# Loading two small projection matrices over other queues: E and F by SyncE and ScalarE in f32, with casts on two engines

## The chip, the cores and the metric

The kernel runs on one core of a Trainium2 chip. A core has five engines that run side by side, each with its own stream of instructions: TensorE (PE, matrix products and transposes into PSUM; PEld is its loading of weights), VectorE (DVE), ScalarE (ACT), GpSimd (POOL) and SyncE (SP). Transfers between memory and the chip are issued by GpSimd, SyncE or ScalarE and carried out by DMA engines. The metric is the device time of one launch in microseconds (us), lower is better; the time before is 431.67 us, the median of 4 runs (431.21 to 432.22).

## The reference

The kernel computes a Linformer attention and feeds its result to an MLP-Mixer block. Sizes: batch 8, 8 heads, sequence 1024, head size 64, projected length 64; the mixer has a token width of 256 and a channel width of 1536.

```python
k_proj = np.einsum('ks,bhsd->bhkd', E, k)        # E: 64 x 1024
v_proj = np.einsum('ks,bhsd->bhkd', F, v)        # F: 64 x 1024
scores = scale * np.matmul(q, k_proj.transpose(0, 1, 3, 2))
attn = softmax(scores)
x = np.matmul(attn, v_proj)                      # heads side by side: (8, 1024, 512)
h = np.maximum(x.T @ w_tok1, 0.0) @ w_tok2       # over the sequence
u = x + h.T
out = u + np.maximum(u @ w_ch1, 0.0) @ w_ch2     # over the channels
```

All inputs and the output are f32. E and F are the same for all batches and heads, so nothing of the attention can begin before both have been loaded and transposed.

## The kernel before, in words

The kernel holds everything in bf16 on chip; GpSimd's transfers change f32 to bf16 on the way. The order of the work on all engines is written out by hand in a long list of step names (ORDER); the program sorts its steps by that list and emits them, so each engine's order is fixed. Transfers are issued ahead of that list, in the order in which the code stands.

The edit is in the opening part of the kernel (lines 184 to 245). There GpSimd issues, one after another: E into partitions 0 to 63 and F into partitions 64 to 127 of one bf16 tile, EF_sb (lines 197 and 198); then, for each of the four head pairs of batch 0, k, q and v of that pair (line 165, 256 KB each as bf16); after the first of these triples it builds the identity matrix that TensorE's transposes need (two instructions from masks.py); after the last the token weights wt1 and wt2 (lines 206 and 207), and then the channel weights and the whole q, k and v of batch 1 (lines 191, 165 and 195). A GpSimd transfer takes one of eight semaphores in turn, so the ninth waits until the first has landed, and so on.

Meanwhile VectorE clears the two block-diagonal tiles kbd and vbd (lines 216 to 219). TensorE multiplies zeros eight times to stay active (busy, line 226), and then runs the first steps of the list:

- EF: eight transposes of EF_sb into PSUM (line 231), and a copy by VectorE into EFT (line 232).
- For head pair hp: KP.hp and VP.hp, the projections of k and v by EFT (lines 240 and 245); KT.hp, the transposes of the projected k (265); QT.hp, the transposes of q (395); S, the scores (449), with their exponential on ScalarE (456); O, the product with the projected v (294), with a reciprocal and a product on VectorE (300, 301). Some KP and VP steps are preceded by filler products (line 431).
- Then the token mixing (464, 477), its transposes (491), and the channel mixing of batch 0 (532).

The copies between these steps are by VectorE or ScalarE (lines 249 and 251), by a list. ScalarE loads its table of functions ahead of its first such copy. From there the batches overlap: while TensorE does the channel mixing of one batch (lines 600 and 655), attention and token mixing of the next are inserted between. Output tiles o1 and o2 have two buffers each and are stored by SyncE (lines 676 and 680).

Of the kernel before, what the change touches and what calls it, by code (L numbers as in the profile page):

```python
# [10 lines left out]
F32 = mybir.dt.float32  # L11
BF16 = mybir.dt.bfloat16
ALU = mybir.AluOpType
ACT = mybir.ActivationFunctionType
# [78 lines left out]
def kernel(  # L93
# [13 lines left out]
    nc = tc.nc  # L107
    P = 128
    B, H, S, D = q.shape
    KP = E.shape[0]  # L110
# [13 lines left out]
    work = ctx.enter_context(tc.tile_pool(name="work", bufs=1))  # L124
# [19 lines left out]
    ident = const.tile([P, P], BF16, name="ident")  # L144
# [6 lines left out]
    kbd = const.tile([P, H, P], BF16, name="kbd")  # L151
# [8 lines left out]
    def load(b, name, src, hs=slice(0, 8)):  # L160
        if hs.start == 0:
            st[name, b] = work.tile(
                [P, H, SC * D], BF16, tag=name + "_sb", name=name + "_sb", bufs=1
            )
        nc.gpsimd.dma_start(
            out=st[name, b][:, hs], in_=src[b, hs].rearrange("h (p si) d -> p h (si d)", p=P)
        )
# [16 lines left out]
    EF_sb = work.tile([P, S], BF16, tag="T1", name="EF_sb", bufs=1)  # L184
# [9 lines left out]
        cs = slice(j * CH, j * CH + CH)  # L194
        nc.gpsimd.dma_start(out=wc2[:, cs], in_=wc2_v[:, cs])

    nc.gpsimd.dma_start(out=EF_sb[0:KP], in_=E)
    nc.gpsimd.dma_start(out=EF_sb[KP:P], in_=F)
    for hp in range(HP):
        hs = slice(2 * hp, 2 * hp + 2)  # L200
        for name, src in ((("k", k), ("q", q), ("v", v))):
            load(0, name, src, hs)
        if hp == 0:
            make_identity(nc, ident)
        if hp == 3:
            nc.gpsimd.dma_start(out=wt1, in_=moe_w_tok1.rearrange("(p si) t -> p si t", p=P))
    nc.gpsimd.dma_start(out=wt2, in_=moe_w_tok2.rearrange("(tc p) s -> p tc s", p=P))
# [13 lines left out]
    def busy(psf, n):  # L221

        zero = kbd.rearrange("p h k -> p (h k)")
        w_ps = psf("w_ps")
        for _ in range(n):
            nc.tensor.matmul(w_ps, zero[:, 0:P], zero[:, 0:512], start=True, stop=True)
# [5 lines left out]
        nc.vector.tensor_copy(out=EFT.rearrange("p s k -> p (s k)"), in_=e_ps)  # L232

    busy(c_ps, 8)


    def k_mm(b, kv_ps, hs, si, f):
# [670 lines left out]
```

## Time and profile before

| | |
|---|---|
| median of 4 runs | 431.67 us |
| the profiled execution | 431.56 us |
| its span on the core | 429.8 us |
| TensorE busy | 415.7 us, 97% of the span |
| VectorE, ScalarE, GpSimd busy | 301.6, 202.4, 206.4 us |
| granted TensorE clock | 1.0 |
| E, F: issue to landing | 3.0 and 3.1 us |

The span runs from the first to the last instruction of the core; the rest of the device time lies around it. The page gives busy time by engine, a picture of the span in 40 slices, and the chain of work that ended last, which is followed back from the last instruction to whatever released each step. In rows of the timeline, the columns are the start, the length, the engine, the line of the code, the operation, the tiles written and read, the size, the count, and in brackets the idle time of the engine before it with what ended that.

### The profile page before, as it was taken

What the parts mean: (1) busy time and instruction counts of PE and PEld (TensorE: products, weight loads), DVE (VectorE), ACT (ScalarE), POOL (GpSimd) and SP (SyncE); (2) the same over time, 40 slices, a digit from 0 to 9 for tenths busy, and PEclk for the clock granted to TensorE, in tenths of its full rate; (3) what the DMA queues carried; (4) which work ended last, traced back from release to release, by engine and by line L of the source; (5) the groups of instructions that cost most, each with busy time, mean ns of one, the idle gap of its engine ahead of it and who ended that gap; (6) DMA issues with size and microseconds to landing.
All of it is one profiled execution on the core that took longest, in us unless ns stands there. A gap on an engine that the chain in (4) does not pass through costs nothing.

```text
span 429.8 us, 7700 instructions
## 1 busy us (share of the span) xinstructions
PE 415.7 (97%) x3034; PEld 271.8 (63%) x3066; DVE 301.6 (70%) x509; ACT 202.4 (47%) x360; POOL 206.4 (48%) x150
## 2 busy tenths in 40 slices
PE   7789999999999999999999999999999999999995
PEld 3577456765478644785467844786458854785585
DVE  2475468768936878867768777777779766947862
ACT  1436684157552556234753366334652356315621
POOL 8350014134652647553565645635356626654652
PEclk9999999999999999999999999999999999999999
DMA  8999999979987999943999289364914320342014
GB/s 123 207 206 206 207 191 172 218 131 219 208 118 177 163 224 179 177 91 58 249 169 206 106 146 153 69 172 103 156 37 99 98 99 2 57 142 98 2 50 146
DMA packets 89332, 60.53 MB, mean 141 GB/s; under 512 B 55760, under 2 KB 84944, under 8 KB 89296
## 3 DMA queue, kind: packets, MB, share of 16 engines
q0 software_dynamic: 29360, 29.63, 44.2%
q1 hardware_dynamic: 59936, 30.42, 30.2%
q8 instruction: 24, 0.39, 0.4%
q14 instruction: 12, 0.10, 0.1%
HBM read 59.24 MB, written 16.78 MB: 177 GB/s over the span
## 4 chain that ended last, share of the span: by engine, by line
PE 90%; DVE 4%; DMA 2%; POOL 2%; issue 1%; ACT 0%; DVEq 0%; ACTq 0%; POOLq 0%
PE be L655 19%; PE be L600 17%; PE ga L655 9%; PE ga L600 9%; PE h_ps L341 5%; PE u_ps L357 5%; PE g_ps L532 5%; PE al L655 4%; PE al L600 4%; PE ou_ps L294 4%; PE kv_ps L240 3%; DMA q_sb<-in_q_dram 2%; PE sco L281 2%; DVE S L524 1%; PE u_ps L477 1%; PE h_ps L464 1%
## 5 line engine op out<-in xcount | busy, mean ns | idle before, releaser
L564 ACT ACTIVATE K<-be 128x512 f32<-128x512 f32 x116 | 65.7, 598 | 66.1 <-PE be L655 38.6
L655 PEld LDWEIGHTS <-g 128*128 128x128 bf16 x768 | 74.5, 98 | 16.1 <-issue 1.0
L655 PEld LDWEIGHTS <-S 128*128 128x128 bf16 x576 | 55.9, 98 | 11.7 <-issue 0.4
L286 ACT ACTIVATE attnT<-sco 128x512 bf16<-128x512 f32 x56 | 33.5, 598 | 50.9 <-PE sco L281 39.3
L600 PEld LDWEIGHTS <-wc 128*128 128x128 bf16 x336 | 32.1, 98 | 36.2 <-issue 0.4
L691 POOL TENSOR_TENSOR K<-K,u_sb 128x512 f32<-128x512 f32 x16 | 19.0, 1185 | 68.7 <-ACT K L564 68.7
L655 PE MATMUL be<-wc,g 128*128 128x256 bf16 x384 | 48.5, 273 | 0.7 <-DVE g L522 0.6
L564 ACT ACTIVATE K<-ga 128x512 f32<-128x512 f32 x58 | 33.0, 601 | 33.6 <-PE ga L655 29.9
L301 DVE TENSOR_TENSOR x_sb<-ou_ps,rdn 128x512 bf16<-128x512 f32 x64 | 44.3, 692 | 2.2
L600 PE MATMUL be<-uT,wc 128*128 128x512 bf16 x168 | 44.7, 379 | 0.2
L360 DVE TENSOR_TENSOR u_sb<-u_ps,x_sb 128x512 bf16<-128x512 f32 x56 | 37.1, 685 | 9.4 <-PE u_ps L357 8.1
L600 PEld LDWEIGHTS <-uS 128*128 128x128 bf16 x252 | 24.0, 98 | 25.7
L606 DVE CUSTOM_DVE_ANT_0 g<-be,K 128x512 bf16<-128x512 f32 x42 | 27.5, 688 | 16.8 <-PE be L600 16.6
L518 POOL TENSOR_TENSOR S<-g 128x1024 bf16<-128x1024 bf16 x7 | 14.9, 2122 | 46.7 <-DVE g L606 46.7
L522 POOL TENSOR_TENSOR g<-g 128x1024 bf16<-128x1024 bf16 x13 | 28.9, 2226 | 14.6 <-DVE S L518 14.4
L639 ACT ACTIVATE g<-be 128x512 bf16<-128x512 f32 x42 | 23.8, 597 | 25.7 <-PE be L600 25.7
L606 DVE CUSTOM_DVE_ANT_0 g<-al,K 128x512 bf16<-128x512 f32 x42 | 27.7, 688 | 10.8 <-PE al L600 10.6
L701 POOL TENSOR_TENSOR K<-K,u_sb 128x512 f32<-128x512 f32 x16 | 20.3, 1270 | 30.0 <-ACT K L564 30.0
L300 DVE RECIPROCAL rdn<-ou_ps 128x8 f32<-128x8 f32 x64 | 13.1, 205 | 25.5 <-PE ou_ps L294 25.0
L357 PE MATMUL u_ps<-R_sb,wt 128*128 128x512 bf16 x104 | 29.9, 379 | 0.6 <-DVE u_sb L360 0.3
L524 POOL TENSOR_TENSOR S<-g,S 128x1024 bf16<-128x1024 bf16 x13 | 28.3, 2183 | 0.9 <-DVE S L520 0.7
L341 PE MATMUL h_ps<-x_sb,wt 128*128 128x512 bf16 x102 | 28.1, 379 | 0.3
(101 smaller groups left out, 774.5 us busy)
## 6 DMA issues: line engine op xcount, KB each, us to landing
out_dram<-o SPq DMA_DIRECT2D x30, 512.0 KB, 3.2
q_sb<-in_q_dram POOLq DMA_DIRECT2D x7, 1024.0 KB, 12.7
k_sb<-in_k_dram POOLq DMA_DIRECT2D x7, 1024.0 KB, 12.5
v_sb<-in_v_dram POOLq DMA_DIRECT2D x7, 1024.0 KB, 12.5
wc<-in_moe_w_ch_dram POOLq DMA_DIRECT2D x4, 384.0 KB, 13.7
wc<-in_moe_w_ch_dram POOLq DMA_DIRECT2D x2, 768.0 KB, 27.4
k_sb<-in_k_dram POOLq DMA_DIRECT2D x4, 256.0 KB, 7.9
q_sb<-in_q_dram POOLq DMA_DIRECT2D x4, 256.0 KB, 8.5
```

What stands on the lines that cost most here:

```text
L286: nc.scalar.activation(out=at, in_=sco, func=ACT.Exp, scale=scale)
L301: nc.vector.tensor_tensor(out=st["x", b][:, :, h * D : (h + 1) * D].rearrange("p (b k) d -> p b k d", b=2), in0=ov[:, :, :, 0:D], in1=rdn[ ...
L341: nc.tensor.matmul(st["h", b], wt1[:, s, t * P : (t + 1) * P], st["x", b][:, s, :], start=(s == 0), stop=(s == SC - 1),)
L357: nc.tensor.matmul(u_ps, wt2[:, t, s::SC], st["R", b][:, t, :], start=(t == 0), stop=(t == TC - 1))
L360: nc.vector.tensor_add(out=st["u", b][:, s, :], in0=u_ps, in1=st["x", b][:, s, :])
L522: eng.tensor_sub(out=a21, in0=a11, in1=a21)
L524: eng.tensor_sub(out=s4, in0=a12, in1=s2)
L564: nc.scalar.activation(out=t, in_=x, func=ACT.Copy)
L600: nc.tensor.matmul(acc, l[:, dc, i * P : (i + 1) * P], r[:, :, dc, :], start=start and dc == 0, stop=stop and dc == 1, skip_group_check=True,)
L606: nc.vector._custom_dve(TENSOR_ADD_SAT, out=o, in0=x, in1=y, s0=3.0e38, s1=0.0)
L639: nc.scalar.activation(out=g_part(b, i + e, 1, 1, 0)[:, 0], in_=be[e], func=ACT.Relu)
L655: nc.tensor.matmul(acc[:, e * HF : (e + 1) * HF], l[:, lc + c, l0 + (2 * j + e) * P : l0 + (2 * j + e + 1) * P], r[:, rc + c, r0 : r0 + HF ...
```

## The change: what it does

E is no longer loaded by GpSimd but by SyncE, and F by ScalarE. Both arrive as f32 in a new tile EF_in, which takes one of the two buffers of the output tile o1. VectorE then casts the rows of E into EF_sb and ScalarE the rows of F. GpSimd begins with k of head pair 0, and builds the identity matrix after the first q instead of after the first v. ScalarE gets a copy of one element ahead of its cast. In the changed program its first instructions are: the issue of F, the load of its table, which waits for nothing, the one-element copy, which waits for the clearing of kbd, and the cast of F, which waits for F.

```diff
-    nc.gpsimd.dma_start(out=EF_sb[0:KP], in_=E)
-    nc.gpsimd.dma_start(out=EF_sb[KP:P], in_=F)
+    EF_in = work.tile([P, S], F32, tag="o1", name="EF_in", bufs=2)
+    nc.sync.dma_start(out=EF_in[0:KP], in_=E)
+    nc.scalar.dma_start(out=EF_in[KP:P], in_=F)
     for hp in range(HP):
         hs = slice(2 * hp, 2 * hp + 2)
         for name, src in ((("k", k), ("q", q), ("v", v))):
             load(0, name, src, hs)
-        if hp == 0:
-            make_identity(nc, ident)
+            if (hp, name) == (0, "q"):
+                make_identity(nc, ident)
...
     busy(c_ps, 8)
+
+    first = work.tile([P, 1], BF16, tag="first", name="first", bufs=1)
+    nc.scalar.activation(out=first, in_=kbd[:, 0, 0:1], func=ACT.Copy)
+    nc.vector.tensor_copy(out=EF_sb[0:KP], in_=EF_in[0:KP])
+    nc.scalar.activation(out=EF_sb[KP:P], in_=EF_in[KP:P], func=ACT.Copy)
```

## The prediction

> **What bounds the kernel now.** The page first: the span is 429.8 us of the profiled execution's 431.56 us, so 1.76 us lie outside it, and TensorE is busy for 415.7 us, 97% of the span, at the full granted clock. The only slices of it below nine tenths are the first three and the last. The edit touches only the first few microseconds, so I asked for the chain of work that ended last over the first 60 us (start, length, piece):
>
> ```profile
> 1.25 0.69 POOL EF_sb L197
> 1.94 0.52 POOL EF_sb L198
> 2.46 0.57 POOL k_sb L165
> ...
> 7.33 0.70 POOL k_sb L165
> 8.02 9.34 DMA q_sb<-in_q_dram
> 17.36 0.05 issue
> 17.41 0.62 PE qt_ps L395 x8
> 18.03 0.16 PE kt_ps L265 x2
> ```
>
> Up to 17.4 us the end is set by loads: GpSimd issues E, F and then the k, q and v of head pairs, and the chain sits on the transfer of the third q piece (head pair 2) until it lands at 17.36. After that it is TensorE almost without a break. So a microsecond won before 17.4 is a microsecond at the end, if TensorE can use the earlier data and nothing later takes it back.
>
> The timeline of TensorE over the same stretch says what it waits for, and with how much spare time:
>
> ```profile
> 5.27 1.01 PE L231 MATMUL e_ps<-ident,EF_sb 128*128 128x128 bf16 x8 [0.22 <-POOL ident masks.py:199]
> 7.07 1.06 PE L240 MATMUL kv_ps<-k_sb,EFT 128*64 128x128 bf16 x8 [0.78 <-DVE EFT L232]
> ...
> 12.28 0.44 PE L240 MATMUL kv_ps<-k_sb,EFT 128*64 128x128 bf16 x5 [0.82 <-DMA k_sb<-in_k_dram]
> ...
> 14.89 0.63 PE L245 MATMUL kv_ps<-v_sb,EFT 128*64 128x128 bf16 x8 [0.56 <-DMA v_sb<-in_v_dram]
> ...
> 16.16 0.61 PE L240 MATMUL kv_ps<-k_sb,EFT 128*64 128x128 bf16 x8 [0.30 <-DMA k_sb<-in_k_dram]
> ```
>
> The transposes of E and F start at 5.27 (their weight load at 5.10). From there to 17.41 TensorE stands waiting for k (0.82 + 0.30), for v (0.56) and, by its weight loads' waits, for q (0.8 in three times): 2.5 us. That is the room in which it can start later, or run earlier.
>
> Last, the stages of the transfers (stretch, then busy time and count of PE, PEld, DVE, ACT, POOL, the clock, the DMA share, GB/s as written):
>
> ```profile
> 2.00:2.50 0.50, 0.50 (x3) 0.16 (x2) 0.13 (x2) 0.50 (x1) 0.50 (x2) 1.00 0.00 0
> 2.50:3.00 0.50, 0.50 (x2) 0.15 (x1) 0.00 (x0) 0.27 (x1) 0.50 (x1) 1.00 0.63 45
> 3.00:3.50 0.50, 0.50 (x2) 0.15 (x1) 0.00 (x0) 0.00 (x0) 0.50 (x2) 1.00 0.98 147
> 3.50:4.00 0.50, 0.50 (x3) 0.16 (x2) 0.00 (x0) 0.00 (x0) 0.50 (x2) 1.00 1.17 180
> 4.00:4.50 0.50, 0.50 (x3) 0.14 (x1) 0.00 (x0) 0.00 (x0) 0.50 (x1) 1.00 1.08 178
> ```
>
> Nothing moves before about 2.65, 1.4 us after GpSimd began its first issue. E and F write 256 KB as bf16: 22 + 74 + 90 KB by 4.0, the rest at 178 GB/s by about 4.4. Only then is the stream free for the first k. From 10 us on it runs at 200 to 210 GB/s without a gap, and each 256 KB piece lands about 1.26 us after the one before it. The loads are one saturated stream, so what starts it earlier should move every landing.
>
> **What the Trainium skill says.** "DMA: Bandwidth & Descriptors", section "Specifications", puts the first byte of a GpSimd transfer at about 1 us and of a SyncE or ScalarE transfer at about 0.6 us; here GpSimd's took 1.4 with the issue, and the other is not shown on loads. The same page, "Issuing engines are not separate DMA queues", says that all of them run on the same 16 DMA engines and that issuing from several saves only sequencer time. So E and F get no bandwidth of their own; the gain can only be that they run while the engines still stand idle.
>
> **The change, part by part.**
>
> 1. *Two issues leave GpSimd* (0.69 + 0.52 us in the chain). The first k is then issued at 1.25 where E was, and data of k, q, v start at about 2.65 instead of 4.4, if E and F are out of the way: at most 1.75 us earlier. Issuing doesn't bind later: one piece costs GpSimd 0.72 us, the transfer 1.26. The wait of GpSimd for an earlier transfer still reaches back eight transfers: the third v still waits for the first k, the fourth k for the first q. Every later wait of this kind keeps its partner.
>
> 2. *E on SyncE, F on ScalarE.* Neither has work: VectorE starts its first instruction at 0.92, and SyncE and ScalarE should be free at about 0.95. SyncE's issues take 0.33 us (median of the stores), so bytes should flow from 0.95 + 0.33 + 0.6 = 1.9 at the latest, 1.55 if the 0.6 runs from the issue's start. Both move 512 KB of f32, which is the amount read before as well. At the 206 GB/s of the saturated stream as written, 412 as read, that is 1.25 us of all engines. Before 2.65 they get 0.75 to 1.1 us of that; 0.15 to 0.5 us remain and delay the first k. So the stream gains 1.75 - 0.5 = 1.25 to 1.75 - 0.15 = 1.6. If the hardware queue is slower to start than I think, E, F and k are interleaved and the gain shrinks to 0. I take 1.3, the lower part, since the early stream (147 to 180) was slower than the later one.
>
> 3. *Landing, casts and the transposes.* SyncE's stores of 512 KB (SBUF to DRAM, the only plain transfers on that queue) give the nearest landing:
>
> ```profile
> DMA to landing us min/median/max: 2.3/3.1/8.0
> ```
>
> So E and F land at about 0.95 + 3.1 = 4.05, perhaps 0.6 earlier as they are half that size. ScalarE: issue to 1.3, table load 1.28 us to 2.6 (before it waited for a memset until 1.48; now it waits for nothing), the 1-element copy, then F: a 1024-wide copy took 1.02 us here, so F is ready at 4.05 + 1.05 = 5.1. "ScalarE: Activation LUTs", "What ACT_TABLE_LOAD costs", gives 0.186 + 0.833 per thousand elements, 1.04, which agrees. VectorE: its memsets end at 2.24; E's cast costs 0.69 by the 2x column of "VectorE: DVE Perf Modes", perf-mode tier table (1.23 for 2048), or 1.2 at the slope of the PSUM casts (0.42 for 256, 0.29 for 128). Ready at 4.75 to 5.3. The identity, now built after two issues, is ready at about 3.3 instead of 5.22. So the transposes start at 4.5 to 5.4, where they start at 5.27 now: no change on this path, and no gain claimed.
>
> 4. *Whether TensorE can use it.* With the transposes as now, it is ready for the second k at 11.46, when its fillers end. That k lands at about 12.2 - 1.3 = 10.9, so this step gains 0.8. The next waits (q 0.4, v 0.56, k 0.30, q 0.2) give up the rest, and at the first step of the third q the shift is the full 1.3: 16.1 in place of 17.41. With no load to wait for it could be there at 17.41 - 2.5 = 14.9, so 1.2 us of room remain.
>
> 5. *What else is added:* the slot of an output tile holds E and F in f32; the first output tile then takes the other slot, with no wait before 79 us. The first copy into the block-diagonal k (ACT, 9.78) now also waits for ScalarE's own earlier work, done by about 5.
>
> After 17.4 TensorE's recorded waits are 3.6 us in all, all on VectorE, 2.3 of them where the attention product waits for its buffer; none is on a load. The token weights land at about 25 to 26, close to their use at 26.14, but they come in the same stream and move with it. The second batch's v lands at about 50.6 against its use at about 52. I give 0.1 for such edges.
>
> Sum: span 429.8 - 1.3 + 0.1 = 428.6; with 1.76 around it 430.36. The profiled execution is 0.11 below the median shown, so against 431.67 the forecast is **430.5**, 0.28% less. About 0.2% (0.86 us) is what a measurement of this kernel can tell from no change.
>
> **The rivals.**
>
> *No gain, the engines are shared (18%).* E's and F's packets first flow at 2.6 and interleave with k: the same bytes stand ahead of the third q, landings move by 0 to 0.6. For it: the stream already uses all 16 engines. Against it: they idle until 2.65. Time 431.1 to 431.7, say 431.4.
>
> *Gained and given back (10%).* A later wait at fixed time takes it up: VectorE's chain from the attention product, at 21.2 and 24.9. Against it: VectorE itself idles ahead of those pieces until TensorE delivers (4.6 us). Time 431.5.
>
> *Slower: E and F come late (10%).* The casts put a new step after landing. The longest landing seen on that queue is 8.0 us; at 0.95 + 8.0 + 1.05 the transposes start at 10.0, 4.7 to 4.9 late, and 2.5 us of room leave a loss of about 2.3: 434.0. It decides from transposes later than 7.7; beyond 8.5 the loss is over 0.86. A milder form: "TensorE: Matmul & The Clock Gate", Part 1, has the array at half clock after an idle window of about 3.4 us; in this trace the 512-wide fillers still take 0.43 us at 8 us and about 0.25 at 10.4, so a long gap before the transposes would add slow matmuls. About 433 for the case.
>
> *As forecast (62%):* 429.8 to 430.9 for itself.
>
> **How the numbers follow.** Faster: nearly all of the forecast's case and a little of the shared one, 0.63. Within 0.2%: most of the shared and the given-back, 0.27. Slower 0.10. The range 429.7 to 431.9 holds the forecast's case, the shared and the given-back; it leaves out the late case and a twentieth at the low end.
>
> **What would show it.** E and F landing at 3.4 to 4.1; F's cast about 1.03 us; transposes at 4.5 to 5.4; the stream at full share from about 2 us; the third q landing at 16.0 to 16.2 and TensorE's chain from 16.1, with every later piece about 1.2 earlier. Wrong if data on the new queues flow only after 2.6, if the transposes start after 7.7, or if the third q moves but not the end.

## The result, and the profile after

The changed kernel takes 430.9 us (median of 37 runs, 430.18 to 432.05) against 431.64 for the kernel before (59 runs, 430.58 to 432.42). The ratio is 0.9988, interval 0.9983 to 0.9993. By the medians that is 0.74 us, by the ratio 0.5 us: a gain clear of noise, in the direction forecast, and about half of the 1.2 us forecast (0.4 to 0.6 of it). The one profiled execution flatters it: 430.27 us, with a span of 428.5, is 1.3 us below the profiled execution before. So two things have to be explained: the 1.3 us in that execution, and why the typical run keeps only about half of it.

The chain of work that ended last, of the changed kernel, over the first 40 us (start, length, piece):

```profile
0.74 4.79 DMA EF_in<-in_E_dram
5.53 0.02 issue
5.55 0.70 DVE EF_sb L239
6.25 0.14 issue
6.38 0.70 PE e_ps L232 x8
...
8.48 1.19 PE w_ps L227 x3
...
10.86 1.52 PE kv_ps L437 x4
...
16.35 0.45 PE qt_ps L401 x8
```

The loads of k, q and v have left the chain. It now runs through the landing of E, 4.8 us after its issue, then VectorE's cast, and from 6.38 on through TensorE alone. TensorE's waits say the same, ahead of the third q (17.6 us, the whole list):

```profile
PE w_ps L227 <- DVE kbd L217: 1.5, 1, 1.5
PE e_ps L232 <- DVE EF_sb L239: 1.3, 1, 1.3
PE kv_ps L246 <- DVE EFT L233: 0.8, 1, 0.8
```

No wait for a load is left, where there were 0.82, 0.56 and 0.30 before. TensorE's timeline, and below it GpSimd's issue that waits for the third q to land:

```profile
6.38 0.69 PE L232 MATMUL e_ps<-ident,EF_sb 128*128 128x128 bf16 x8 [1.33 <-DVE EF_sb L239]
7.85 0.63 PE L246 MATMUL kv_ps<-k_sb,EFT 128*64 128x128 bf16 x8 [0.78 <-DVE EFT L233]
8.42 1.26 PE L227 MATMUL w_ps<-kbd 128*128 128x512 bf16 x3
...
10.65 1.73 PE L437 MATMUL kv_ps<-EFT,ident 128*128 128x512 bf16 x4
...
16.18 0.61 PE L401 MATMUL qt_ps<-ident,q_sb 128*128 128x128 bf16 x8
```

```profile
16.27 0.74 POOL L191 DMA_DIRECT2D wc<-in_moe_w_ch_dram  x1 [0.48 <-DMA q_sb<-in_q_dram]
```

The transposes start at 6.38 in place of 5.27, the transposes of the third q at 16.18 in place of 17.41: 1.1 later, then 1.2 earlier. In the kernel before, that issue of GpSimd began at 17.64, 0.28 after the landing at 17.36; here the third q thus landed at about 16.0, and TensorE took it up 0.2 later. Four fillers that took 1.03 us before take 1.73 here. They start 0.43 apart, where in the kernel before it was 0.22: half speed. The stretches show the clock (the number after the five engines is the granted TensorE clock, then the DMA share and GB/s written):

```profile
2.00:2.50 0.50, 0.50 (x3) 0.15 (x2) 0.13 (x2) 0.50 (x1) 0.50 (x2) 1.00 1.10 115
2.50:3.00 0.50, 0.50 (x2) 0.15 (x1) 0.00 (x0) 0.32 (x2) 0.50 (x2) 1.00 0.52 197
3.00:3.50 0.50, 0.50 (x2) 0.15 (x1) 0.00 (x0) 0.00 (x0) 0.42 (x3) 1.00 1.14 328
3.50:4.00 0.50, 0.50 (x3) 0.15 (x2) 0.00 (x0) 0.00 (x0) 0.50 (x1) 1.00 0.98 229
4.00:4.50 0.50, 0.50 (x3) 0.14 (x1) 0.00 (x0) 0.03 (x1) 0.50 (x2) 1.00 0.95 199
...
9.00:10.00 1.00, 1.00 (x6) 0.30 (x5) 0.00 (x0) 0.01 (x1) 0.46 (x2) 0.50 1.21 199
10.00:11.00 1.00, 1.00 (x9) 0.81 (x8) 0.10 (x1) 0.54 (x2) 0.63 (x1) 0.50 1.25 208
11.00:12.00 1.00, 1.00 (x4) 0.30 (x2) 0.59 (x1) 0.00 (x0) 0.72 (x1) 0.50 1.23 204
12.00:13.00 1.00, 1.00 (x18) 0.69 (x16) 0.00 (x0) 0.01 (x1) 0.57 (x1) 0.97 1.25 206
```

Two readings. From 2.0 to 4.5 about 534 KB are written, and E and F are 524 KB of f32: so they fill the engines until about 4.5, and the first k flows no earlier than before. The packets of each queue in the trace say it directly: F's run from 2.1 to 3.6, E's from 3.3 to 4.7, and the first of k moves at 4.39, where it was 4.36 in the kernel before. And the clock falls to a half from 8.7 to 12.1. It is recorded only from its first change on; the eight zero products from 1.46 ran at half speed too (0.43 us apart), though the column says 1.00 there.

The runs of the changed kernel fall in groups by their mean recorded clock: 21 of 38 with 0.995 or 0.996 take 430.18 to 430.93, 14 with 1.0 take 431.19 to 432.05, and 3 with 0.992 take 431.7 to 431.9. (One execution more has its clock on record than the 37 of the median.) A mean of 0.996 over 428.5 us is one stretch of 3.4 us at half clock, as in the profile above. A mean of 1.0 isn't a run without half clock: it only says that the clock never fell back. The half clock of the start is not counted, however long it lasts.

### The profile page after: what moved, and what is told of

Read it like the earlier page. It is cut to its first block, busy times and chain, and to the rows that moved or that the text cites. A ratio compares the mean times of both kernels' runs of the same rounds, so it can differ in the third digit from the quotient of the medians.

```text
span 428.5 us, 7705 instructions
## 1 busy us (share of the span) xinstructions
PE 415.2 (97%) x3034; PEld 271.1 (63%) x3066; DVE 302.7 (71%) x510; ACT 203.4 (47%) x362; POOL 205.5 (48%) x148
## 4 chain that ended last, share of the span: by engine, by line
PE 92%; DVE 4%; DMA 1%; issue 1%; POOL 0%; ACT 0%; DVEq 0%; ACTq 0%
PE be L661 19%; PE be L606 17%; PE ga L661 9%; PE ga L606 9%; PE h_ps L347 5%; PE u_ps L363 5%; PE g_ps L538 5%; PE al L661 4%; PE al L606 4%; PE ou_ps L300 4%; PE kv_ps L246 4%; PE sco L287 2%; DMA EF_in<-in_E_dram 1%; DVE S L530 1%; PE qt_ps L401 1%; PE u_ps L483 1%
## 5 line engine op out<-in xcount | busy, mean ns | idle before, releaser
L612 DVE CUSTOM_DVE_ANT_0 g<-al,K 128x512 bf16<-128x512 f32 x42 | 27.7, 688 | 10.4 <-PE al L606 10.2
## 6 DMA issues: line engine op xcount, KB each, us to landing
wc<-in_moe_w_ch_dram POOLq DMA_DIRECT2D x4, 384.0 KB, 14.3
```

The source lines that it names most:

```text
L612: nc.vector._custom_dve(TENSOR_ADD_SAT, out=o, in0=x, in1=y, s0=3.0e38, s1=0.0)
```

## The experiments

The theory: E lands late, TensorE idles ahead of and after the transposes, and the clock, which in the profile changes after stretches of 3.4 us, leaves or puts the array at half clock until 12 us or later in part of the runs, as these stretches fall differently from run to run; those runs lose what the loads gained. The rivals: the spread comes from later in the kernel; or the late transposes cost by themselves.

### The kernel before, again

No edit.

> The kernel before, unchanged, for the clock and time of each of its runs. Theory (the clock): in the changed kernel TensorE idles 1.3 us ahead of the transposes and 0.8 us after them, because E lands late; depending on where the activity windows of the clock (3.4 us each in the trace) fall, the array then stays at half clock until about 12 or later, and the runs fall in two groups, about 430.5 and 431.6. The kernel before idles only 0.2 us ahead of the transposes, so it should show one mean clock (1.0) in nearly all runs and one group around 431.6. Rival (something later): the spread comes from later in the kernel and has nothing to do with the front; then the kernel before shows the same two groups, about 1.1 us apart, in like shares.

Measured: 431.48 us (14 runs), its companion runs 431.5 (35 runs, 5 of them below 431.0). The mean clocks spread from 0.992 to 1.0, so the expectation of one clock fell: the front's clock varies in the kernel before too. Its times don't form two groups, though. Its profile, TensorE:

```profile
8.46 1.01 PE L240 MATMUL kv_ps<-k_sb,EFT 128*64 128x128 bf16 x8 [2.16 <-DMA k_sb<-in_k_dram]
...
11.84 1.91 PE L431 MATMUL kv_ps<-EFT,ident 128*128 128x512 bf16 x4
...
17.55 0.61 PE L395 MATMUL qt_ps<-ident,q_sb 128*128 128x128 bf16 x8
```

Here the first k was taken up 1.4 us later than in the other profile and the fillers were slow, and yet the third q is transposed at 17.55, only 0.14 later than in the profile shown with the prediction. In the kernel before TensorE had that room, since the third q lands at about 17.4 in both profiles.

### The changed kernel, again

No edit.

> The changed kernel unchanged, for another profile and more runs by clock. The groups come back: about 430.5 where the mean clock is 0.995 or 0.996, about 431.6 where it is 1.0, median 430.6 to 431.2. Should the profile fall in the 1.0 group, TensorE is at half clock until 12.5 to 13.8 and reaches the third q at 17.0 to 17.5 though it has landed by 16.7.

Measured: 430.93 us (14 runs). Seven runs with 0.995 or 0.996 take 429.94 to 430.82, five with 1.0 take 431.03 to 432.23, one each with 0.992 and 0.999 take 432.2 and 432.0. The profile fell in the first group again (third q at 16.11), so the 1.0 group of the changed kernel itself was not seen in a trace. The nearest to it is a version with the same instructions on TensorE and a short memset on GpSimd (told below): its profile has a mean of 1.0, half clock from the start until 12.9, and the third q at 17.11, though it had landed at about 16.4 (0.28 ahead of the second line):

```profile
17.11 0.61 PE L403 MATMUL qt_ps<-ident,q_sb 128*128 128x128 bf16 x8
```

```profile
16.72 0.74 POOL L191 DMA_DIRECT2D wc<-in_moe_w_ch_dram  x1 [0.47 <-DMA q_sb<-in_q_dram]
```

### TensorE kept busy

```diff
-    busy(c_ps, 8)
+    busy(c_ps, 11)
...
         nc.vector.tensor_copy(out=EFT.rearrange("p s k -> p (s k)"), in_=e_ps)
+        busy(c_ps, 2)
```

> The changed kernel with 3 more zero products ahead of the transposes (11 in place of 8) and 2 after them, so that TensorE has no long gap until 8 us. E lands as late as before, the transposes start at about 6.4. Theory (the clock): full clock from about 5 to 9 us on and no return to half; one group at about 430.3 to 430.6, median 430.4, 0.5 below the changed kernel. Rival (something later): median 430.9, two groups as in the changed kernel. Second rival (the late transposes cost by themselves): 430.9, since they are as late as before.

Measured: 429.97 us, all six runs 429.26 to 430.52; ratio to the kernel before 0.9965 (0.9951 to 0.9979). The upper group is gone with five products of zeros added to the program, and the median is 0.4 below the expectation. Nothing was taken away, and the transposes began at 6.19, so E is about as late; both rivals fall. This is a faster kernel than the two compared here.

With only the first half of that edit (11 products, none after the transposes):

> The changed kernel with the 3 more zero products ahead of the transposes and none after them. If the gap ahead of the transposes is the one that counts, 430.0 as with both; if both gaps count, runs fall in two groups again, with a median of 430.2 to 430.6.

Measured: 430.04 us, all 15 runs 429.41 to 430.98; ratio 0.997 (0.9961 to 0.9979). The gap ahead of the transposes is the one that counts; what the other two products add, 0.07, is within the noise.

### TensorE idle for longer

```diff
-    busy(c_ps, 8)
+    busy(c_ps, 4)
```

> The changed kernel with 4 zero products in place of 8 at the start, so that TensorE idles about 3 us ahead of the transposes in place of 1.3. Theory (the clock): no early full clock in any run, one group at the slow end, 431.5 to 432.0, and the group at 430.5 is gone. If the clock of the front isn't what divides the runs, the median stays at 430.9 with two groups, since no load and no wait is touched.

Measured: 431.8 us (13 runs, 430.83 to 432.7, two below 431.0; 0.9 above the changed kernel); ratio to before 1.0006 (0.9996 to 1.0016). The whole gain is gone, though no load and no wait was touched. Its profile and that of the version with 11 products are the cleanest pair of all. TensorE with 4 products:

```profile
6.38 1.04 PE L232 MATMUL e_ps<-ident,EF_sb 128*128 128x128 bf16 x8 [3.04 <-DVE EF_sb L239]
...
9.20 1.46 PE L227 MATMUL w_ps<-kbd 128*128 128x512 bf16 x3
...
10.81 1.04 PE L401 MATMUL qt_ps<-ident,q_sb 128*128 128x128 bf16 x8
...
17.08 0.61 PE L401 MATMUL qt_ps<-ident,q_sb 128*128 128x128 bf16 x8
```

TensorE with 11 products:

```profile
6.68 0.71 PE L232 MATMUL e_ps<-ident,EF_sb 128*128 128x128 bf16 x8 [0.34 <-ACT EF_sb L240]
...
8.75 0.82 PE L227 MATMUL w_ps<-kbd 128*128 128x512 bf16 x3
...
9.66 0.62 PE L401 MATMUL qt_ps<-ident,q_sb 128*128 128x128 bf16 x8
...
15.43 0.62 PE L401 MATMUL qt_ps<-ident,q_sb 128*128 128x128 bf16 x8
```

And GpSimd's issue that waits for the third q, with 4 products and then with 11:

```profile
15.45 0.74 POOL L191 DMA_DIRECT2D wc<-in_moe_w_ch_dram  x1 [0.47 <-DMA q_sb<-in_q_dram]
```

```profile
15.67 0.74 POOL L191 DMA_DIRECT2D wc<-in_moe_w_ch_dram  x1 [0.47 <-DMA q_sb<-in_q_dram]
```

In the first the data were there 0.2 us earlier and the transposes began 0.3 earlier, yet TensorE took up the third q 1.65 us later: from the transposes on the instructions are the same, but at half clock until 12.9 in place of 6.7. The spans are 429.4 and 427.6.

### No wait for E and F

```diff
-    nc.vector.tensor_copy(out=EF_sb[0:KP], in_=EF_in[0:KP])
-    nc.scalar.activation(out=EF_sb[KP:P], in_=EF_in[KP:P], func=ACT.Copy)
+    nc.vector.memset(EF_sb, 0.03125)
```

> The changed kernel with the two casts left out: the tile that is transposed is filled with a constant by VectorE, so the transposes wait for neither E nor F (both are still transferred); the projections are not those of the reference. Theory (the clock): transposes at about 5.1, loads as in the changed kernel, the third q at 16.1, about 430.3. Second rival (late transposes): the same 430.3, so this run bounds what the lateness of E costs in all. Rival (something later): 430.9.

Measured: 429.88 us, all six runs 429.24 to 430.15. The version with both fillers stands 0.1 above this one, in which the transposes began at 4.85. So with the clock out of the way, transposes at 6.2 to 6.7 cost next to nothing, as the prediction's room of 2.5 us said.

### The fillers in the kernel before

Here 9 products in place of 8, and the 2 after the transposes.

> The kernel before with one more zero product ahead of the transposes (9 in place of 8) and 2 after them, nothing else. If the half clock of the front costs the kernel before as well, and the earlier stream of loads is a gain of its own, this lies between: about 431.0 to 431.3, narrower than the kernel before (430.4 to 432.4), and the changed kernel with its fillers (429.97) stays about 1.1 to 1.3 below it. If all of that version's 1.5 came from the fillers, this one reaches 430.0 too. If the clock matters only where E comes late, it stays at 431.5.

Measured: 431.44 us (13 runs, 430.84 to 431.85), the kernel before beside it 431.43; ratio 1.0004 (0.9996 to 1.0012). It is narrower and no faster. Its profiled execution was at half clock from 9.2 to 12.6, so these fillers didn't keep every run at full clock; but there TensorE still waits for the loads (0.30 ahead of the third k), with the third q at 17.27. So fillers alone gain nothing in the kernel before, and the 1.4 us between it and the changed kernel with 11 products belong to the change.

### Where the earlier loads come from

In the changed kernel, a memset of 1 us on GpSimd ahead of the first k (in the slot of an output tile):

```diff
+    idle = work.tile([P, 1024], F32, tag="o2", name="idle", bufs=2)
+    nc.gpsimd.memset(idle, 0.0)
```

> The changed kernel with a memset of about 1 us on GpSimd ahead of the first k, so that the issue time saved is spent again, while E and F run on the idle engines. If E is late because the first k and q share the engines with it, E and F now land at 3.4 to 4.2 and the transposes start at about 5.1. If the earlier stream is what gives the gain, the third q lands about 1.0 later than in the changed kernel, at 17.1, and the time is 431.3. If it is not, and the late E is what costs, the time is 430.3 to 430.5.

It is inconclusive: GpSimd could start the memset at 0.74, where its first issue otherwise starts at 1.25, so that the first k was only 0.38 late. Measured 431.17 us, with the same two groups as the changed kernel (10 of 22 runs at 430.31 to 430.77, the others 431.13 to 432.27), since nothing was done for the clock. The later of E and F still landed only at 5.3, and at 5.4 in the next run, where k was issued 1.4 us later than in the changed kernel; in neither did a packet of k move before 4.18. So sharing with k isn't what makes the second of them late.

With two such memsets, and 11 products so that the clock matters less:

> The changed kernel with 11 zero products (no early idle of TensorE) and two memsets of about 0.95 us each on GpSimd ahead of the first k, which is then issued at about 2.5, as late as in the kernel before. If what the loads gain is the earlier issue by GpSimd, it is gone: the third q lands at 17.2 to 17.5, 431.3. If it is that E and F are carried while the engines are idle and no longer stand in GpSimd's own queue, the first k still starts when E and F are through (about 4.4) and the time stays at 430.0 to 430.5.

Measured: 430.82 us (14 runs, 430.16 to 431.35); ratio 0.999 (0.9982 to 0.9998). GpSimd, in its profile:

```profile
2.64 0.86 POOL L165 DMA_DIRECT2D k_sb<-in_k_dram  x1
```

Between the two expectations: of the 1.4 us the early issue is worth 0.8 (430.82 less 430.04), and 0.6 remain with k issued as late as before. The 0.8 is not an earlier start of the data: the first packet of k moved at 4.24 here, and at 3.90 to 4.39 where k was issued at 1.25. The stream after it was slower in the two profiles (183 against 197 GB/s from 4.5 to 9 us); why is not shown.

Then E and F by GpSimd again, as f32, with the casts and 11 products kept:

```diff
-    nc.sync.dma_start(out=EF_in[0:KP], in_=E)
-    nc.scalar.dma_start(out=EF_in[KP:P], in_=F)
+    nc.gpsimd.dma_start(out=EF_in[0:KP], in_=E)
+    nc.gpsimd.dma_start(out=EF_in[KP:P], in_=F)
```

> The changed kernel with 11 zero products, but E and F issued by GpSimd ahead of the first k again, as f32 into the same tile, with the casts kept. This keeps everything but the queue and the issue time. In four profiles with E and F cast by GpSimd's own transfers the chip moved 137 to 162 GB/s from 4.5 to 9 us, in six with E and F on the other queues 158 to 203. If standing in GpSimd's queue is what slows the stream, it is slow again: 140 to 165 GB/s, the third q's transposes at 17.3, 431.3. If the issue time alone counts (k at about 2.45), it is like the version with the late k, 430.8. If neither, 430.0.

Measured: 431.22 us (14 runs, 430.99 to 432.49); ratio 1.0001 (0.9993 to 1.0008). One stretch of its profile, and the same stretch of the version with the late k:

```profile
4.50:9.00 4.50, 0.94 1.13 155
```

```profile
4.50:9.00 4.50, 1.00 1.18 183
```

With k issued at nearly the same time (2.47 and 2.64), the loads run at 155 GB/s where E and F stood in GpSimd's queue and at 183 where they didn't. Over all profiles this stretch had 137, 143, 150, 155 and 162 with E and F issued by GpSimd, and 158 to 203 (mean 184 of eight) with them on the other queues. What in that queue slows the early stream stays open. This version's transposes also came late, at 7.20, and its profile was at half clock for a while, so the 0.4 us between it and the late k are not the queue's alone.

### The rest of the change alone

The identity after the first q, and ScalarE's one-element copy with its table load, in the kernel before.

> The kernel before with only the rest of the change: the identity built after the first q in place of the first v, and ScalarE's one-element copy with its table load ahead; E and F stay with GpSimd. The table load ended at 2.76 and its first use came at 9.78, and the identity ended at 5.22 against E and F at 5.05, so nothing is to be won: 431.3 to 431.6, the same as the kernel before.

Measured: 431.43 us (14 runs) beside 431.4; ratio 0.9996 (0.9986 to 1.0005). The table load began at 0.74 in place of 1.48 and nothing followed from it.

## Why the prediction was right and wrong

The direction held and the median lies in the range; the size was 1.2 us where 0.5 to 0.74 were measured.

*The end follows the third q.* Right. The span less the start of that step is 412.4 and 412.3 us in the two kernels, and 412.2 to 412.7 in every profile of the experiments. Nothing later took more than 0.3 back; the rival "gained and given back" is out, and so is the 0.1 set aside for it.

*Step 1 and 2, the stream starts 1.25 to 1.6 us earlier.* Wrong in its mechanism, nearly right in its amount, and that by luck. SyncE and ScalarE issued at 0.74, earlier than the 0.95 taken, but each issue took 0.57 in place of 0.33, and the first packet moved at 2.09, 0.8 after the issue ended, where the step had added 0.6. E and F then took until about 4.6: 524 KB in 2.5 us, 210 GB/s as written. I had costed f32 at the 412 GB/s that the casting transfers read, 1.25 us for both. So the idle time ahead of 2.65 took only about an eighth of them (66 KB), and k's data began at 4.39, as before (4.36), and not 1.25 to 1.6 earlier. The stream gained after that: 193 in place of 162 GB/s from 4.5 to 9. By the filled versions, in which the loads set the pace, it is worth 1.4 us (431.43 to 430.04), against 1.3 taken. Of this, 0.8 hang on GpSimd's earlier issue, by a way that is not shown.

*Step 3, E and F land at about 4.05 and the transposes start at 4.5 to 5.4.* This is the step that failed. I had priced each landing by the stores' 3.1, as if neither transfer delayed the other. The two moved one after the other and landed 3.7 and 4.8 us after issue: E's first packet moved at 3.3, as F's were ending, and each landed 0.8 to 0.9 after its last packet. F was there first, so ScalarE's cast (1.05, as taken) was done by 5.5; E's came at 5.55 and took 0.69, as the step had estimated. Transposes at 6.38, outside the stated bounds of 4.5 to 5.4.

*Step 4, TensorE has 2.5 us of room.* True in instructions and false in clock. A start 1.1 us late was within the room, as the run without the wait showed (0.1 us between). But the room had been read from a trace in which TensorE reached full clock at 10.2. I had named the clock, and had put it with the slower case as a mild addition to a start that comes very late; an idle time of 1.3 us was enough. With TensorE at half clock until 12 us or longer it is the bound in place of the loads: in the profile the third q is taken up at 16.18, close to the forecast of 16.1, but that is luck too: it had landed at 16.0, and what held it was TensorE and not a load. Against the 430.0 of the filled version, 21 of 38 runs stand at about 430.5 and lose 0.5, the other 17 stand near 431.6 and lose about 1.6, which is all that the loads had won. (Of the upper runs no trace was taken; that they were at half clock is read from their mean clock and from the profiles of the versions with the memset and with 4 products.)

*The rivals.* "Slower, E and F come late" had the cause and the wrong price: it asked for transposes after 7.7, and the harm came at 6.4 by the way that the milder form names. "No gain, the engines are shared" was right that k does not start earlier, but not by interleaving (no packet of k moved before 4.39), and wrong on the outcome. More than issue time was saved, which the prediction had not expected of shared engines: 0.6 of the 1.4 us stayed with k issued as late as before.

On the clock, "TensorE: Matmul & The Clock Gate", Part 1, says that it falls back after an idle window of about 3.4 us. The traces agree on the window (the stretches at 1.0 and then 0.5 last 3.4 us each) but not on idleness: in the stretch before the fall, 5.25 to 8.66, TensorE worked from 6.38 to 7.07 and from 7.85 on, 1.5 of 3.4 us. It was enough to be half idle. The other profiles agree: full clock was lost after stretches with 1.2 to 1.6 us busy (this kernel again, the filled kernel before, E and F by GpSimd) and kept after 2.5 to 2.6 (no wait, 11 products, late k). To get it took more: it came after stretches with 3.1 us busy or more, and did not after one with 3.0 (the kernel before with the rest of the change, 7.44 to 10.86; stretches ahead of the first record are counted back in steps of 3.41 us). These are one profile each, so the bounds are rough.

## What to carry to other kernels

Where the opening of a kernel waits for a transfer, what the wait does to TensorE's clock can cost more than the wait: keep TensorE busy right up to the first real product, and when an edit makes that product later, lengthen the filler with it. Room read from a trace holds only for the clock of that trace, so look at how the runs group by clock before you spend it. A load in f32 over another queue is not costed by what the casting transfers read; its own bytes written per microsecond and its landing have to be measured.

## What was not expected of the hardware

Two loads of 256 KB, issued at the same time by SyncE and ScalarE, first moved data 1.3 us after issue began, and one landed about 1.1 us after the other in nearly every profile (3.7 and 4.8 us), sometimes E first, sometimes F; only in the version with both fillers were they close, at 4.2 and 4.3. A kernel of 430 us shows groups of runs 1.1 us apart from a clock that, in every profile, is at full from 14.3 us on, but for the last 1.4 us of the span. The same loads at the same place run at 137 to 203 GB/s in the stretch from 4.5 to 9 us, from one execution to another, and part of that follows which queue E and F had been on.
